# A fused attention and feed-forward kernel on one core: the second product with its operands exchanged and its output transposed

## The chip, the core and the metric

The kernel runs on one core of one Trainium2 chip. The metric is the device time of one execution in microseconds; the median of several runs is compared. What the host does with the arrays before and after the launch isn't part of it.

## What is computed

For 8 batches of 8 heads, 576 tokens and 64 dimensions, an attention without softmax is followed by a norm over each head's 64 values and by a gated feed-forward layer. The 4,608 tokens have 512 values each (8 heads of 64), and the hidden layer has 2,048:

```
kv  = einsum('bhsd,bhse->bhde', k, v)
out = einsum('bhsd,bhde->bhse', q, kv)
x   = out / sqrt(mean(out*out, -1) + 1e-6) * g_norm      # then (b s) x (h d): 4608 x 512
h   = x @ w_in                                           # 4608 x 2048
g   = h * (1 / (1 + exp(-h)))
return g @ w_out                                         # 4608 x 512, float32
```

The weights reach the device as 64-bit words, two 32-bit integers per value, and the kernel makes float32 from them itself.

## The kernel before, in words

**Tiles.** Tokens come in 9 tiles (`NT`) of `TN` = 512. The model's 512 columns (`DM`) are `NP` = 4 pieces of 128, the hidden layer's 2,048 are `NF` = 16 pieces of 128. One step is one pair (token tile `t`, hidden piece `f`); there are 144 of them.

**Precision by parts.** TensorE multiplies `F32R` tiles, each value of which is a rounded float32. Every operand of the two large products is kept as a high part and a low part (the rest), and a product is the sum of three matmuls: high by high, high by low and low by high. For the weights `split_block` (L163) makes the parts: the high one by a ScalarE copy (L166) into `w[:, 0, :]`, the low one by a GpSimd subtraction (L167) into `w[:, 1, :]`. `bits` (L124) before it makes float32 values from the words on VectorE.

**First product**, `products` (L503): for each of the 4 pieces of the model's columns, three matmuls (L507) with a 128 by 128 piece of w_in stationary and 512 tokens of x^T moving (`xl`, then `xh` twice). Twelve matmuls add up in one PSUM bank `hp`: 128 hidden units by 512 tokens.

**Gate**, `gate` (L512): ScalarE reads `hp` twice, into `gh` (F32R, L516) and `gf` (float32, L517), and the low part `gl` = gf - gh is made on VectorE (on GpSimd in the first token tile, L518). Both tiles hold 128 hidden units by 512 tokens.

**Second product**, `project` (L532): for each of four blocks of 128 tokens (`ns`) three matmuls (L537), with 128 columns of `gh`, `gh` and `gl` stationary, and the 512 columns of w_out's piece moving (low part, high part, high part). They add up in the block's own bank `acc`, 128 tokens by 512 columns, over the 16 hidden pieces; so four banks are open through a token tile. These three matmuls are called a group here; a step has four groups. After the last hidden piece the bank is copied to SBUF (`ob`, L542, by ScalarE for odd blocks and VectorE for even ones), and SyncE's queue stores it (L543). In the last token tile the last bank is split into two of 256 columns, one of them from another PSUM pool (`sums_of`, L523), so that the end is shorter.

**Order.** The order is written out by hand (`tc.manual_schedule`). Each step runs, in order: the conversion of weights that falls due (in the first token tile only), the first product, the gate, pieces of the attention for the following batch (`mid_jobs`, L246 and L277 to L279 on TensorE), the second product of the step two before (`LAG` = 2, L727 to L730), and more of the attention. So TensorE takes turns between L507 and L537, with short attention matmuls between in about a third of the steps. After the loop the last two steps' second products are run bank by bank (L733 to L735). Loads and stores all stand in SyncE's queue.

Of the kernel before, what the change touches and what calls it, by code (L numbers as in the profile page):

```python
# [8 lines left out]
F32 = mybir.dt.float32  # L9
# [22 lines left out]
def linear_attention_rms_silu_ffn(  # L32
# [17 lines left out]
    nc = tc.nc  # L50
    B, H, S, D = q.shape
    DM, FF = w_in.shape
    P = 128
    NP = H // 2
    NF = FF // P
    TN = 512
# [14 lines left out]
    ps_acc = ctx.enter_context(tc.tile_pool(name="ps_acc", bufs=4, space=PSUM))  # L71
# [245 lines left out]
    class FirstPair:  # L317
# [43 lines left out]
        def make_out(self):  # L361
            self.ps = self.ps or acc_bank()
            for r in range(4):
                w = slice(r * P, (r + 1) * P)
                nc.tensor.matmul(out=self.ps[:, w], lhsT=self.qT[:, w], rhs=self.kvm, start=True, stop=True)
# [20 lines left out]
    class Rest:  # L386
# [8 lines left out]
        def turn_q(self):  # L395
            self.halves = acc_bank()[0:D, :].rearrange("d (c h n) -> d h c n", h=2, n=64)
            for h in range(2):
                for c in range(NP):
                    nc.tensor.transpose(
                        out=self.halves[:, h, c, :], in_=self.q[:, 2 * c + h, :], identity=ident[:64, :64]  # L400
                    )
# [89 lines left out]
        return ps_h.tile([P, 512], F32, name="hp", tag="h")  # L491

    def acc_bank():
        return ps_acc.tile([P, DM], F32, name="acc", tag="acc")

    at_tags = ["at"]

    def at_bank(tag=None):

        at_tags.append(at_tags.pop(0))  # L500
        return ps_at.tile([P, 512], F32, name="at", tag=tag or at_tags[-1])
# [20 lines left out]

    def sums_of(t):  # L523

        whole, half = slice(0, DM), (slice(0, DM // 2), slice(DM // 2, DM))
        banks = [(acc_bank(), n, whole) for n in range(TN // P)]
        if t == NT - 1:
            last, n, _ = banks.pop()
            banks += [(last, n, half[0]), (at_bank(), n, half[1])]
        return banks  # L530

    def project(t, f, gh, gl, bank, n, cs):  # L532
        w = parts["wo", f]
        ns = slice(n * P, (n + 1) * P)
        bank = bank[:, :cs.stop - cs.start]
        for i, (g, a) in enumerate(((gh, 1), (gh, 0), (gl, 0))):
            nc.tensor.matmul(  # L537
                out=bank, lhsT=g[:, ns], rhs=w[:, a, cs], start=(f == 0 and i == 0), stop=(f == NF - 1 and i == 2)
            )
        if f == NF - 1:  # L540
            ob = tmp.tile([P, S], F32, name="ob", tag="tmp")[:, :cs.stop - cs.start]
            (nc.scalar.copy if n % 2 else nc.vector.tensor_copy)(out=ob, in_=bank)  # L542
            nc.sync.dma_start(out=out[t * TN + n * P:t * TN + (n + 1) * P, cs], in_=ob)  # L543


    first_jobs, mid_jobs, last_jobs, chains = {}, {}, {}, {}
# [38 lines left out]
    with tc.manual_schedule():  # L585
# [4 lines left out]
        for item in ORDER.split():  # L590
            kind, n = item.rstrip("0123456789"), int(item.lstrip("wioqkvbg") or 0)
# [107 lines left out]
        pend, prepped = [], []  # L699
        for t in range(NT):  # L700
            sums = sums_of(t)
            if t == 1:
                at_tags.append("other")
            for f in range(NF):
                g = t * NF + f
                for job in first_jobs.pop(g, ()):
                    job()
                for item in prepped:
                    split_block(*item, nc.scalar.copy)
                prepped = []  # L710
                if t == 0:
                    prepped = [("wi", f + 2)] * (3 <= f + 2 < NF) + [("wo", f)] * (f > 0)
                run(sum((bits(*item) for item in prepped), []), *[call() for call in chains.pop(g, ())])
                if t == 0:
                    for item in [("wi", f + 3)] * (3 < f + 3 < NF) + [("wo", f + 1)] * (1 < f + 1 < NF):
                        magnitude(*item)
                if t == 0 and f < WARM:
                    hp = warm[f]
                    products(hp, t, f, NP - 1)
                else:  # L720
                    hp = h_bank()
                    for c in range(NP):
                        products(hp, t, f, c)
                pend.append(((t, f, *gate(t, hp)), sums))
                for job in mid_jobs.pop(g, ()):
                    job()
                if len(pend) > LAG:  # L727
                    item, olds = pend.pop(0)
                    for old in olds:
                        project(*item, *old)  # L730
                for job in last_jobs.pop(g, ()):
                    job()
        for old in sums:  # L733
            for item, _ in pend:
                project(*item, *old)  # L735


_INS = ["q", "k", "v", "g_norm", "moe_w_in", "moe_w_out"]
_OUT = ((4608, 512), "float32")


# [19 lines left out]
```

## Time and profile before

| | |
|---|---|
| median of 3 runs | 893.68 us (893.66 to 894.28) |
| profiled execution, device time | 893.95 us |
| its span, first to last instruction | 892.1 us |
| mean granted TensorE clock | 0.992 |
| matmuls of the first product (L507) / of the second (L537) | 1,728 / 1,776 |
| stores of the output | 37 |
| bytes read / written in HBM | 45.09 MB / 9.44 MB |

How to read it: PE is TensorE's matmuls and PEld its loads of the stationary operand, which run beside each other; DVE is VectorE, ACT ScalarE, POOL GpSimd and SP SyncE. A row of a group gives line, engine, operation, output <- inputs, the tile size (rows and columns of the array, then output partitions by columns), the count, busy time in us, the mean of one in ns and the idle time before. In such a row `gh` and `gl` stand for the gated units, `wo` for w_out's pieces, `wi` for w_in's, `xh` and `xl` for x^T. A matmul's row lasts until its last column has drained, so that the next one starts before it ends: rows of about 390 ns follow each other every 230 ns or so. The granted clock is the share of TensorE's full speed.

### The profile page before, as it was taken

The page shows a single profiled execution, that of the slowest core. Times are in us where ns is not written, and L with a number is a line of the kernel's source. Part 1 is how long each engine was busy: PE and PEld are TensorE (multiplying, and loading weights), DVE is VectorE, ACT ScalarE, POOL GpSimd, SP SyncE. Part 2 cuts the span into 40 slices and gives each one's busy share as a digit, 9 for nine tenths or more (in the row PEclk, how much of TensorE's full clock was granted, in tenths as well). Part 3 has the DMA queues.
Part 4 walks back from the last instruction along what each step waited for, and adds up shares of the span by engine and source line. Part 5 has one row for each costly group of instructions (what it writes and reads, how often), then busy time and mean ns, then how long its engine had stood idle before and what let it go on. Part 6 is the DMA issues. An engine that isn't in the chain of part 4 may idle for free.

```text
span 892.1 us, 11345 instructions
## 1 busy us (share of the span) xinstructions
PE 871.0 (98%) x4438; PEld 713.1 (80%) x4438; DVE 337.7 (38%) x617; ACT 307.5 (34%) x684; POOL 176.8 (20%) x172
## 2 busy tenths in 40 slices
PE   7879989999999999999999999999999999999998
PEld 6658868888888888888888888888888888888887
DVE  5888894233232423341433233332523141111111
ACT  4567634332343224322432243322432231112121
POOL 1489963101120002101210112010310020000000
PEclk9899989999999999999999999999999999999999
DMA  9869402310052004300431024100400010001001
GB/s 243 257 212 326 117 0 80 87 41 1 11 148 49 0 1 128 80 1 1 116 65 28 1 71 96 41 1 1 127 1 1 1 47 1 1 1 48 0 1 48
DMA packets 108389, 55.26 MB, mean 62 GB/s; under 512 B 76464, under 2 KB 101808, under 8 KB 108336
## 3 DMA queue, kind: packets, MB, share of 16 engines
q1 hardware_dynamic: 108336, 54.54, 22.5%
q8 instruction: 35, 0.57, 0.3%
q14 instruction: 18, 0.15, 0.1%
HBM read 45.09 MB, written 9.44 MB: 61 GB/s over the span
## 4 chain that ended last, share of the span: by engine, by line
PE 87%; DMA 3%; DVE 3%; POOL 3%; issue 2%; SPq 1%; ACT 0%; DVEq 0%; POOLq 0%
PE hp L507 41%; PE acc L537 40%; PE at L246 2%; DMA early_wo<-in_q 1%; DMA wi<-in_moe_w_in 1%; DMA wo<-in_moe_w_out 1%; POOL wi L167 1%; PE at L278 1%; PE at L279 1%; PE at L277 1%; POOL full L120 1%; PE at L537 1%; DMA kv<-in_k 1%; DVE m L476 1%; POOL wo L167 1%
## 5 line engine op out<-in xcount | busy, mean ns | idle before, releaser
L507 PE MATMUL hp<-xh,wi 128*128 128x512 f32 x1144 | 355.4, 392 | 2.1 <-POOL wi L167 2.1
L537 PE MATMUL acc<-wo,gh 128*128 128x512 f32 (+1 forms) x1152 | 355.3, 390 | 1.4 <-POOL wo L167 1.4
L518 DVE TENSOR_TENSOR gl<-gf,gh 128x512 fp32r<-128x512 f32 x128 | 88.6, 692 | 500.5 <-ACT gf L517 500.5
L507 PEld LDWEIGHTS hp<-xh,wi 128*128 128x128 f32 x1144 | 215.9, 189 | 46.0 <-POOL wi L167 3.2
L537 PEld LDWEIGHTS acc<-wo,gh 128*128 128x128 f32 x1152 | 214.8, 188 | 45.8 <-POOL wo L167 1.8
L507 PE MATMUL hp<-xl,wi 128*128 128x512 f32 x572 | 227.8, 398 | 3.5 <-ACT wi L166 3.5
L516 ACT ACTIVATE gh<-hp 128x512 fp32r<-128x512 f32 x143 | 85.5, 598 | 416.8 <-PE hp L507 416.6
L537 PE MATMUL acc<-wo,gl 128*128 128x512 f32 x576 | 222.5, 386 | 0.0
L507 PEld LDWEIGHTS hp<-xl,wi 128*128 128x128 f32 x572 | 108.0, 189 | 26.8 <-ACT wi L166 3.9
L537 PEld LDWEIGHTS acc<-wo,gl 128*128 128x128 f32 x576 | 108.2, 188 | 23.8
L313 POOL TENSOR_TENSOR xl<-o,xh 128x448 fp32r<-128x448 f32 (+7 forms) x56 | 53.2, 951 | 343.5 <-ACT xh L312 343.5
L517 ACT ACTIVATE gf<-hp 128x512 f32<-128x512 f32 x143 | 84.6, 592 | 0.0
L267 POOL TENSOR_TENSOR ql<-qT,qh 128x576 fp32r<-128x576 f32 x28 | 40.1, 1431 | 177.0 <-ACT qh L266 88.5
L283 ACT ACTIVATE sq<-at 128x288 f32<-128x288 f32 x56 | 23.2, 415 | 39.4 <-PE at L279 26.8
L253 ACT COPY kvm<-at 64x64 f32<-64x64 f32 x56 | 11.6, 207 | 59.4 <-PE at L246 59.1
L304 DVE SCALAR_TENSOR_TENSOR o<-o,gcol,yT 128x448 f32<-128x448 f32 (+7 forms) x56 | 31.2, 557 | 2.0
L246 PEld LDWEIGHTS at<-kv 128*64 128x64 f32 (+1 forms) x560 | 20.8, 136 | 12.0 <-issue 9.7
L246 PE MATMUL at<-kv 128*64 128x64 f32 (+1 forms) x560 | 26.5, 231 | 0.0
L312 ACT CAST xh<-o 128x448 fp32r<-128x448 f32 (+7 forms) x56 | 24.8, 442 | 5.0 <-DVE o L304 5.0
L297 DVE STREAM_TRANSPOSE yT<-y 128x448 f32<-128x448 f32 (+7 forms) x56 | 25.9, 463 | 0.0
L167 POOL TENSOR_TENSOR wi<-full,wi 128x512 fp32r<-128x512 f32 x16 | 21.4, 1334 | 21.2 <-ACT wi L166 21.2
L284 ACT COPY o<-at 128x288 f32<-128x288 f32 x56 | 22.7, 406 | 4.0 <-POOL xl L313 4.0
(104 smaller groups left out, 514.5 us busy)
## 6 DMA issues: line engine op xcount, KB each, us to landing
out<-ob SPq DMA_DIRECT2D x35, 256.0 KB, 2.1
wi<-in_moe_w_in SPq DMA_DIRECT2D x16, 512.0 KB, 6.4
wo<-in_moe_w_out SPq DMA_DIRECT2D x16, 512.0 KB, 11.1
qt<-in_q SPq DMA_DIRECT2D x112, 72.0 KB, 3.7
kv<-in_k SPq DMA_DIRECT2D x28, 256.0 KB, 3.1
kv<-in_v SPq DMA_DIRECT2D x28, 256.0 KB, 3.6
kv<-in_k SPq DMA_DIRECT2D x28, 32.0 KB
kv<-in_v SPq DMA_DIRECT2D x28, 32.0 KB
```

The source lines that it names most:

```text
L167: nc.gpsimd.tensor_tensor(out=w[:, 1, :], in0=full, in1=w[:, 0, :].bitcast(F32), op=ALU.subtract)
L246: nc.tensor.matmul(out=self.kv[h], lhsT=self.k[rows, c, :], rhs=self.v[rows, c, :], start=(r == 0), stop=(r == 4))
L267: nc.gpsimd.tensor_tensor(out=self.ql, in0=self.qT, in1=self.qh.bitcast(F32), op=ALU.subtract)
L297: nc.vector.transpose(out=self.yT.rearrange("p (j a) -> p j a", a=32), in_=y[:, a // 32:e // 32].unsqueeze(2).to_broadcast([P, (e - a) // ...
L304: nc.vector.scalar_tensor_tensor(out=self.o[:, a:e], in0=self.o[:, a:e], scalar=gcol, in1=self.yT, op0=ALU.mult, op1=ALU.mult)
L312: nc.scalar.copy(out=th[:, self.c, w], in_=self.o[:, a:e])
L313: nc.gpsimd.tensor_tensor(out=tl[:, self.c, w], in0=self.o[:, a:e], in1=th[:, self.c, w].bitcast(F32), op=ALU.subtract)
L507: nc.tensor.matmul(out=hp[:, :TN], lhsT=w[:, a, fs], rhs=x[:, c, :], start=(c == 0 and i == 0), stop=(c == NP - 1 and i == 2),)
L516: nc.scalar.activation(out=gh, in_=hp[:, :TN], func=AF.Silu)
L517: nc.scalar.activation(out=gf, in_=hp[:, :TN], func=AF.Silu)
L518: (nc.gpsimd if t == 0 else nc.vector).tensor_tensor(out=gl, in0=gf, in1=gh.bitcast(F32), op=ALU.subtract)
L537: nc.tensor.matmul(out=bank, lhsT=g[:, ns], rhs=w[:, a, cs], start=(f == 0 and i == 0), stop=(f == NF - 1 and i == 2))
```

## The change

In the second product the operands change places. A 128 by 128 piece of w_out (high, low, high) is stationary, and the 512 tokens of `gh`, `gh` and `gl` move. A bank now holds 128 of the model's columns by 512 tokens, so the output tensor on the device is out^T, 512 by 4,608; the stores write 128 rows of 512 tokens into it, and the host's code turns the array. The order of the three matmuls in a group changes as well: the high part of w_out is used first and the low part second. In the last token tile the split bank is split by tokens in place of by columns.

```diff
     def acc_bank():
-        return ps_acc.tile([P, DM], F32, name="acc", tag="acc")
+        return ps_acc.tile([P, TN], F32, name="acc", tag="acc")
...
     def sums_of(t):
 
-        whole, half = slice(0, DM), (slice(0, DM // 2), slice(DM // 2, DM))
-        banks = [(acc_bank(), n, whole) for n in range(TN // P)]
+        whole, half = slice(0, TN), (slice(0, TN // 2), slice(TN // 2, TN))
+        banks = [(acc_bank(), n, whole) for n in range(NP)]
...
-        for i, (g, a) in enumerate(((gh, 1), (gh, 0), (gl, 0))):
+        for i, (g, a) in enumerate(((gh, 0), (gh, 1), (gl, 0))):
             nc.tensor.matmul(
-                out=bank, lhsT=g[:, ns], rhs=w[:, a, cs], start=(f == 0 and i == 0), stop=(f == NF - 1 and i == 2)
+                out=bank, lhsT=w[:, a, ns], rhs=g[:, cs], start=(f == 0 and i == 0), stop=(f == NF - 1 and i == 2)
             )
         if f == NF - 1:
             ob = tmp.tile([P, S], F32, name="ob", tag="tmp")[:, :cs.stop - cs.start]
             (nc.scalar.copy if n % 2 else nc.vector.tensor_copy)(out=ob, in_=bank)
-            nc.sync.dma_start(out=out[t * TN + n * P:t * TN + (n + 1) * P, cs], in_=ob)
+            nc.sync.dma_start(out=out[ns, t * TN + cs.start:t * TN + cs.stop], in_=ob)
...
-_OUT = ((4608, 512), "float32")
+_OUT = ((512, 4608), "float32")
...
-    return r.results[0]["out_0"]
+    return np.ascontiguousarray(r.results[0]["out_0"].T)
```

## The prediction

> **What bounds the kernel now.** I read the page first, its busy times and its chain, then the groups of both products, then busy times by stretch, and last the waits of TensorE.
>
> ```profile
> span 892.1 us, 11345 instructions
> PE 871.0 (98%) x4438; PEld 713.1 (80%) x4438; DVE 337.7 (38%) x617; ACT 307.5 (34%) x684; POOL 176.8 (20%) x172
> PE 87%; DMA 3%; DVE 3%; POOL 3%; issue 2%; SPq 1%; ACT 0%; DVEq 0%; POOLq 0%
> ```
>
> TensorE is busy 871.0 of 892.1 us and owns 87% of the chain that ended last. Nothing else is busy over 40%, save PEld, which runs beside PE. The program ran 893.95 us in this execution, 1.85 more than its span. The median of the runs shown is 893.68, so the profiled one is 0.27 long. Whether those 98% hold at every place is read by stretch (columns: length, busy us and instructions of each engine, granted clock, DMA share, GB/s):
>
> ```profile
> 0.00:63.00 63.00, 49.19 (x326) 38.45 (x327) 47.51 (x83) 35.17 (x75) 28.73 (x35) 0.95 0.89 248
> 63.00:128.00 65.00, 61.52 (x323) 50.02 (x321) 57.95 (x88) 38.68 (x81) 54.63 (x54) 0.99 0.50 156
> 128.00:134.00 6.00, 5.45 (x13) 3.88 (x14) 5.83 (x9) 3.20 (x6) 5.02 (x5) 0.51 0.00 0
> 134.00:809.00 675.00, 675.00 (x3386) 553.19 (x3385) 215.33 (x424) 213.94 (x492) 88.42 (x81) 1.00 0.16 42
> 809.00:892.10 83.10, 79.84 (x397) 67.52 (x395) 11.07 (x16) 16.54 (x31) 0.00 (x0) 1.00 0.05 17
> ```
>
> From 134 to 809 us TensorE has not one idle nanosecond: 675.00 of 675.00, at full clock. Before 134 it has gaps, and there the weights' conversion on VectorE and GpSimd decides. The chain in order of time shows it just ahead of 128 us:
>
> ```profile
> 108.32 3.56 DVE m L476
> 120.30 1.24 DVE y L200
> 127.78 1.28 POOL wi L167
> 129.11 5.01 PE hp L507 x11
> ```
>
> PE takes the chain over only at 129.11. What it saves before that is waited away at its longest wait (3.5 us, its products on the ScalarE copy of a w_in piece). So a change of TensorE's pace counts from about 129 us to the end, and there nanosecond for nanosecond.
>
> **The change part by part.** *Number of instructions.* Each group was three matmuls of 512 columns with three weight loads (gh, gh, gl stationary, w_out's piece moving). It stays three of 512 columns with three loads (high, low, high piece of w_out stationary, gh, gh, gl moving). The tile sizes are all 128 by 512, d_model being 512 as TN is. So x4438 stays on PE and on PEld, and nothing is gained or lost by counting.
>
> *Pace of one group.* The two products already do the same amount of work per matmul, one with weights stationary (L507) and one with gated units stationary (L537). Here they are in a steady stretch, 700 to 800 us (busy us, then mean ns of one):
>
> ```profile
> L537 PE MATMUL acc<-wo,gh 128*128 128x512 f32 x150 | 46.7, 393 | 0.0
> L507 PE MATMUL hp<-xh,wi 128*128 128x512 f32 x144 | 44.3, 389 | 0.0
> L537 PE MATMUL acc<-wo,gl 128*128 128x512 f32 x75 | 29.1, 388 | 0.0
> L507 PE MATMUL hp<-xl,wi 128*128 128x512 f32 x72 | 28.0, 389 | 0.0
> ```
>
> A group of the second product is 393 + 393 + 388 = 1174 ns of these, a group of the first 3 x 389 = 1167: **7 ns dearer**. These durations overlap (a matmul ends after the next has begun), so I check with busy time, overlaps counted once, over 98.40 us, which are 18 whole steps. The first row is L537 alone, the second L507 alone:
>
> ```profile
> 699.63:798.03 98.40, 52.38 (x216) 40.57 (x216) 1.00 0.03 11
> 699.63:798.03 98.40, 51.86 (x217) 40.54 (x216) 1.00 0.03 11
> ```
>
> 52.38 - 51.86 = 0.52 us over 18 x 4 = 72 groups is 7.2 ns a group, the same. Both products issue 216 loads of equal busy time there (40.57 and 40.54), so it is not the load itself that is longer. The one difference that I see inside a group is that L537 loads the same stationary tile twice running (gh, gh); L507 alternates high, low, high. The changed L537 alternates as L507 does, with pieces of the same layout. I therefore take L507's pace for it: 7 ns less per group.
>
> *How often.* From 134 us to the end:
>
> ```profile
> L537 PE MATMUL acc<-wo,gh 128*128 128x512 f32 x1016 | 316.5, 393 | 0.0
> L537 PE MATMUL acc<-wo,gl 128*128 128x512 f32 x508 | 197.7, 389 | 0.0
> L537 PE MATMUL acc<-wo,gh 128*128 128x256 f32 x32 | 6.3, 279 | 0.0
> L537 PE MATMUL at<-wo,gh 128*128 128x256 f32 x32 | 6.3, 279 | 0.0
> ```
>
> 508 groups of 512 columns (1016 gh, 508 gl): 508 x 7 = 3.56 us. The last token tile's split bank makes 32 groups of 256 columns; no row shows that shape with weights stationary. Between nothing and the same 7 ns that is 0 to 0.22 us, and I take 0.1. **Sum: -3.66 us.**
>
> *The unknown: gated units as moving operand.* No row shows it. From below: were every matmul as short as the shortest 512-column row (388), a group would be 1164, 10 less than now, -5.1 us. From above: were every one as long as the longest (393), 1179, 5 more than now, +2.5 us. I take 389, as the row nearest in form is L507's, which streams 512 contiguous fp32 values from SBUF, written by ScalarE, past weight pieces.
>
> *Waits.* The wait for gh and gl moves from the weight load to the matmul, and the wait for w_out's halves from the matmul to the load. Behind a waiting one on PE's queue stands the rest of the second product and the next step's first product, and the gate waits for that. Neither wait bites in the steady part:
>
> ```profile
> 504.00 0.60 ACT L516 ACTIVATE gh<-hp 128x512 fp32r<-128x512 f32 x1 [4.14 <-PE hp L507]
> 505.11 0.69 DVE L518 TENSOR_TENSOR gl<-gf,gh 128x512 fp32r<-128x512 f32 x1 [4.03 <-ACT gf L517]
> 514.73 0.62 PE L537 MATMUL acc<-wo,gh 128*128 128x512 f32 x2
> ```
>
> With LAG 2, gl is done at 505.80 and used from 514.73: 8.9 us of cover. Were that cover gone, each step could lose at most what gate and subtraction take, 504.00 to 505.80, 1.8 us. In the first token tile the high half, which ScalarE makes, is now needed first and GpSimd's low half one matmul later:
>
> ```profile
> PE acc L537 <- POOL wo L167: 1.4, 1, 1.4
> PE hp L507 <- ACT wi L166: 3.5, 1, 3.5
> ```
>
> This shortens the one wait of 1.4 us by a matmul's pace (98.40 us / 432 = 0.23 us). It lies before 129 us, so what is late next is the 3.5 us wait, and it counts as nothing (0 to 0.23).
>
> *Copies, stores, queues.* Four evacuations a tile on VectorE and ScalarE keep their size. Each store still moves 128 rows of 2,048 bytes (1,024 in the halves), the rows now 18,432 bytes apart in the output. SP's queue issues as many. Only the last store stands on the path:
>
> ```profile
> 888.88 0.37 ACT L542 COPY ob<-at 128x256 f32<-128x256 f32 x1 [0.28 <-PE at L537]
> out<-ob SPq DMA_DIRECT2D x2, 128.0 KB, 1.8
> out<-ob SPq DMA_DIRECT2D x35, 256.0 KB, 2.1
> ```
>
> I take 1.8 us again for it; twice the bytes took 0.3 us more, so a spread-out target should cost some tenths at most. It could be up to 0.3 dearer, or as much cheaper. The turn of the output is made on the host, outside the measured time.
>
> Forecast: 893.95 - 3.66 = 890.29 for an execution like the profiled one; less its 0.27, **890.0 us**.
>
> *A page that speaks against it.* The Trainium skill, "TensorE: Matmul & The Clock Gate", section Back-to-back issue gap, gives a warm matmul's spacing by its moving columns alone, 512 / 2.4 + 2.5, an estimate of 215.8 ns, whichever operand is stationary. By that rule swapping operands of equal size changes nothing. The trace has 228 ns for the mean spacing and the 7 ns between two products of one size, so the rule does not hold to that precision here.
>
> **The rivals.** *No change, 893.7 us.* The 7 ns belong to something that stays. L537 goes to another PSUM bank after every three matmuls, L507 after twelve. Or gh as an operand costs 4 ns on either side, two of three matmuls each time: 508 x 7 ns stays. For it: the bank hop is the second thing that distinguishes the two lines. Against it: at each step PE also hops from acc to hp, and the products' group holds 3 x 389 all the same. It has 0.21. The page's rule gives the same time.
>
> *Slower, 896.2 us.* The 7 ns are the price of reading the gated units' tiles. These now stream through whole, 512 columns three times a group, where before 128 columns a time were loaded. If each of the three then costs the longest row, 393, a group is 1179: 508 x 5 ns = +2.5 us. If the price went by bytes, four times 7 = 28 ns a group, 21 more than now, +10.7 us, 904.4. It decides from 7 ns a group above L507, where it eats the whole gain. Against it: gl lies in the same pool and its row is the shortest, 388. It has 0.12.
>
> *The half clock.* The wait at 127.8 us is followed by the stretch at 0.51 clock:
>
> ```profile
> 130.55 1.05 PE L507 MATMUL hp<-xh,wi 128*128 128x512 f32 x2
> ```
>
> Two matmuls take 1.05 us there against 0.62 in the steady rows, 0.43 us more, half of it a later start and half a longer end, so about 0.2 us of pace each: some 12 of them are 2.4 us. PE comes to this wait a little earlier (13 steps x 4 x 7 ns = 0.36 us). A second such stretch would give 892.4 (0.04); none, 887.6 (0.03). The Trainium skill, same page, section "What's actually happening", has the clock halved after an idle window of about 3.4 us that runs free; the 3.5 us wait followed by 0.51 agrees.
>
> **How the numbers follow.** Forecast 0.60 (its own range 889.3 to 891.0), no change 0.21, slower 0.12, one more half-clock stretch 0.04, one less 0.03. About 0.2% (1.8 us) is what a measurement of this kernel can tell from no change. Faster by more, under 891.9: 0.60 + 0.03 = 0.63. Within: 0.21 + 0.04 = 0.25. Slower: 0.12. The range takes in both ends of the unknown: 893.68 - 5.1 = 888.6 and 893.68 + 2.5 = 896.2; so 888.5 to 896.3, with only a price by bytes and a vanished half-clock stretch outside.
>
> **What would show it.** Right: L537's 512-column rows all read 389 or 390 in the steady stretch, whichever of gh and gl moves; L537's busy time over 18 steps falls from 52.38 to about 51.86; 134 to 809 us stays full and comes to hold some 3 us more of the program; the counts stay x4438. Wrong: rows of 393, 393, 388 again mean that bank hop or operand made them; rows above 393 that moving gated units are dear. New idle time of PE at L537 with ACT or DVE as releaser would mean that the moved wait bites. A last store that lands later than 1.8 us would show in the tail, after the last matmul.

## The result, and the profile after

The changed kernel takes 902.35 us (median of 6 runs, 900.84 to 903.64) against 893.67 us before (6 runs, 892.25 to 894.98): a ratio of 1.0097, 95% interval 1.0082 to 1.0113. It is about 1% slower, where 0.4% faster was forecast.

The page of the changed kernel, its profiled execution at 903.08 us:

```profile
span 901.3 us, 11344 instructions
PE 878.7 (97%) x4438; PEld 712.0 (79%) x4438; DVE 338.1 (38%) x617; ACT 307.2 (34%) x684; POOL 176.2 (20%) x172
PE 88%; DVE 5%; DMA 3%; POOL 1%; issue 1%; SPq 0%; ACT 0%; DVEq 0%; POOLq 0%; ACTq 0%
```

The counts are the same to the last matmul and load, and PE is as much the bound as it was. The 9.2 us of span are therefore in PE's pace or in its gaps. The same stretches as before:

```profile
63.00:128.00 65.00, 63.56 (x329) 51.09 (x327) 55.71 (x84) 39.43 (x83) 52.11 (x51) 1.00 0.51 155
128.00:134.00 6.00, 3.31 (x8) 2.41 (x9) 5.72 (x9) 3.19 (x6) 4.33 (x5) 0.74 0.00 0
134.00:809.00 675.00, 675.00 (x3353) 546.79 (x3352) 215.44 (x424) 212.01 (x490) 90.18 (x83) 1.00 0.16 41
```

From 134 to 809 us PE is full again, 675.00 of 675.00 at full clock, but it starts 3,353 matmuls there in place of 3,386. No wait came in; each matmul takes longer. The rows of the steady stretch, 700 to 800 us, say which:

```profile
L507 PE MATMUL hp<-xh,wi 128*128 128x512 f32 x146 | 45.4, 391 | 0.0
L537 PE MATMUL acc<-gh,wo 128*128 128x512 f32 x144 | 45.2, 394 | 0.0
L507 PE MATMUL hp<-xl,wi 128*128 128x512 f32 x73 | 28.5, 391 | 0.0
L537 PE MATMUL acc<-gl,wo 128*128 128x512 f32 x72 | 28.4, 394 | 0.0
```

All three matmuls of the second product now read 394, where 393, 393 and 388 stood, and L507, which nobody touched, reads 391 in place of 389. Such a row ends after the next has begun, so the pace is better read from starts. Rows of the changed kernel's order of time (start, length):

```profile
706.83 0.63 PE L537 MATMUL acc<-gh,wo 128*128 128x512 f32 x2
...
709.63 0.39 PE L507 MATMUL hp<-xl,wi 128*128 128x512 f32 x1
...
712.37 0.40 PE L537 MATMUL acc<-gh,wo 128*128 128x512 f32 x1
```

And of the kernel before:

```profile
699.63 0.62 PE L537 MATMUL acc<-wo,gh 128*128 128x512 f32 x2
...
702.38 0.39 PE L507 MATMUL hp<-xl,wi 128*128 128x512 f32 x1
...
705.10 0.39 PE L537 MATMUL acc<-wo,gh 128*128 128x512 f32 x1
```

The twelve matmuls of the second product take 709.63 - 706.83 = 2.80 us, 233.3 ns each, and the first product's twelve 2.74 us; before it was 2.75 and 2.72. Over 18 steps the second product's start comes every 99.72 / 18 = 5.540 us, where it came every 98.40 / 18 = 5.467. Finer, by the starts of each matmul: a group of the second product is 700 ns (687 before), and the first product loses 20 ns at its start, where its second to fifth spacings are 236, 228, 232 and 231 ns in place of 226.7. So a plain step, one without attention matmuls, loses 4 x 13 + 20 = 72 ns (73 by the rounded 5.540 and 5.467).

The chain in order of time tells when PE takes over, first after, then before:

```profile
129.87 1.29 POOL wi L167
131.20 4.21 PE hp L507 x11
135.41 2.81 PE acc L537 x12
```

```profile
134.12 2.07 PE acc L537 x9
```

135.41 - 134.12 = 1.3 us are lost ahead of the steady part. From there to the end it is 901.3 - 135.41 = 765.9 us against 892.1 - 134.1 = 758.0, 7.9 more. By the starts of the rows from the fourteenth second product on, 6.0 of these are the second product's and 1.8 the first's; attention and end have 0.1.

### The profile page after: what moved, and what is told of

The parts are those of the page before. It is cut to its first block, busy times and chain, and to the rows that moved or that the text cites. A ratio compares the mean times of both kernels' runs of the same rounds, so it can differ in the third digit from the quotient of the medians.

```text
span 901.3 us, 11344 instructions
## 1 busy us (share of the span) xinstructions
PE 878.7 (97%) x4438; PEld 712.0 (79%) x4438; DVE 338.1 (38%) x617; ACT 307.2 (34%) x684; POOL 176.2 (20%) x172
## 4 chain that ended last, share of the span: by engine, by line
PE 88%; DVE 5%; DMA 3%; POOL 1%; issue 1%; SPq 0%; ACT 0%; DVEq 0%; POOLq 0%; ACTq 0%
PE hp L507 42%; PE acc L537 41%; PE at L246 3%; DMA early_wo<-in_q 1%; DMA wi<-in_moe_w_in 1%; DMA kv<-in_v 1%; PE at L279 1%; PE at L278 1%; PE at L277 1%; DVE full L158 1%; DVE m L476 1%; PE at L537 1%; DVE conv L155 0%; POOL wi L167 0%; DVE full L139 0%
## 5 line engine op out<-in xcount | busy, mean ns | idle before, releaser
L507 PE MATMUL hp<-xh,wi 128*128 128x512 f32 x1144 | 357.6, 394 | 2.3 <-POOL wi L167 2.3
L537 PE MATMUL acc<-gh,wo 128*128 128x512 f32 (+1 forms) x1152 | 358.2, 391 | 0.9 <-POOL wo L167 0.9
L507 PEld LDWEIGHTS hp<-xh,wi 128*128 128x128 f32 x1144 | 216.6, 190 | 47.8 <-POOL wi L167 3.3
L537 PEld LDWEIGHTS acc<-gh,wo 128*128 128x128 f32 x1152 | 214.4, 188 | 50.1 <-POOL wo L167 1.2
L507 PE MATMUL hp<-xl,wi 128*128 128x512 f32 x572 | 228.4, 399 | 3.7 <-ACT wi L166 3.3
L537 PE MATMUL acc<-gl,wo 128*128 128x512 f32 x576 | 225.4, 391 | 0.0
L507 PEld LDWEIGHTS hp<-xl,wi 128*128 128x128 f32 x572 | 108.1, 189 | 27.9 <-ACT wi L166 3.7
L537 PEld LDWEIGHTS acc<-gl,wo 128*128 128x128 f32 x576 | 107.9, 187 | 25.6
```

Source lines behind the costliest of these rows:

```text
L507: nc.tensor.matmul(out=hp[:, :TN], lhsT=w[:, a, fs], rhs=x[:, c, :], start=(c == 0 and i == 0), stop=(c == NP - 1 and i == 2),)
L537: nc.tensor.matmul(out=bank, lhsT=w[:, a, ns], rhs=g[:, cs], start=(f == 0 and i == 0), stop=(f == NF - 1 and i == 2))
```

## The experiments

**The theories.** The prediction's two explanations were the repeated stationary tile and the bank hop; it had the gated units' tiles themselves as a rival. A fourth came after the result and stands in no row of the trace: the *place* of the operands in SBUF. By the addresses that the program is built with, w_in's and w_out's pieces and x^T start 192 bytes past a multiple of 512 in each partition, and gh and gl start 128 past. So the first product reads two operands in line (difference of moving and stationary start 0), the second product before had +64 (w_out's pieces moving), and the changed one has -64. Below, "in line" means a difference of 0 modulo 512: the 128-column pieces of a stationary tile lie 512 bytes apart, so 512 is taken as the period. Whether a shorter one would do, 256 above all, was not tried for a whole product.

**1. The gated units in line.** The changed kernel, with

```diff
+    pad = ctx.enter_context(tc.tile_pool(name="pad", bufs=1))
     gp = ctx.enter_context(tc.tile_pool(name="gp", bufs=LAG + 1))
...
+    nc.gpsimd.memset(pad.tile([P, 16], F32, name="space"), 0.0)
```

> The changed kernel with 64 unused bytes per partition put ahead of the gated units' tiles, so that gh and gl start 192 bytes past a multiple of 512, as w_out's pieces and x^T do, in place of 128 past. In the changed kernel a steady step lasts 5.540 us, its second product 2.800 (233.3 ns a matmul) and its first 2.740. If the address of the moving tile relative to the stationary one sets the pace, the second product falls to about 2.720 us (226.7 ns a matmul, the first product's pace), the step to about 5.44 us, and the whole by some 12 us to about 890 us. If bank hops, the repeated use of the same moving tile, or the place of the tiles at the high end of SBUF set it, all stays: 2.800, 5.540 and about 902 us.

It took 891.18 us, beside 892.56 for the kernel before on the same chip. The rows of 700 to 800 us (L539 is the second product, two lines further down):

```profile
L509 PE MATMUL hp<-xh,wi 128*128 128x512 f32 x150 | 46.2, 389 | 0.0
L539 PE MATMUL acc<-gh,wo 128*128 128x512 f32 x145 | 44.7, 389 | 0.0
L509 PE MATMUL hp<-xl,wi 128*128 128x512 f32 x75 | 29.2, 389 | 0.0
L539 PE MATMUL acc<-gl,wo 128*128 128x512 f32 x73 | 28.4, 389 | 0.0
```

Four times 389: 64 unused bytes make gated units as cheap to move as x^T. In order of time:

```profile
705.52 0.39 PE L509 MATMUL hp<-xl,wi 128*128 128x512 f32 x1
...
708.24 0.62 PE L539 MATMUL acc<-gh,wo 128*128 128x512 f32 x2
...
710.96 0.39 PE L509 MATMUL hp<-xl,wi 128*128 128x512 f32 x1
```

2.72 us for each product: the first one's 20 ns have gone as well.

**2. No bank hops.** The changed kernel, in which a step's four groups add up in one bank, `first` taking the place of `f == 0` as the start of a sum; the sums go to the wrong blocks.

```diff
-    def project(t, f, gh, gl, bank, n, cs):
+    def project(t, f, gh, gl, bank, n, cs, first=None):
+        first = f == 0 if first is None else first
...
-                    for old in olds:
-                        project(*item, *old)
+                    for j, old in enumerate(olds):
+                        if item[0] < NT - 1 and item[1] < NF - 1:
+                            project(*item, olds[item[1] % 4][0], *old[1:], first=(item[1] < 4 and j == 0))
+                        else:
+                            project(*item, *old)
```

> The changed kernel, but in each step but a tile's last the four groups of the second product add up in one PSUM bank (the step's number modulo four), so that twelve matmuls in a row write one bank as in the first product; the sums go to the wrong blocks, the work and the number of matmuls stay. The last token tile is as it was. If the hop to another bank after three matmuls costs the time, the second product falls from 2.800 to about 2.72 us a step in the first eight tiles and the whole by about 11 us. If the moving tile's address or its place costs it, nothing changes: 2.800 us a step and about 902 us.

901.43 us, and the same rows as the changed kernel:

```profile
L538 PE MATMUL acc<-gh,wo 128*128 128x512 f32 x146 | 45.8, 394 | 0.0
L538 PE MATMUL acc<-gl,wo 128*128 128x512 f32 x73 | 28.8, 394 | 0.0
```

The bank hop costs nothing here.

**3. x^T moves in the second product.** The changed kernel, with the result of the gate unused:

```diff
-        for i, (g, a) in enumerate(((gh, 0), (gh, 1), (gl, 0))):
+        mh, ml = xh[t][:, 0, :], xl[t][:, 0, :]
+        for i, (g, a) in enumerate(((mh, 0), (mh, 1), (ml, 0))):
```

> The changed kernel, but the second product's moving operand is the first 512 columns of x^T (high, high, low part) in place of gh, gh, gl; the gate still runs, its result is not used. The same three tiles still repeat in all four groups, and the bank hops stay. If the address or the place of the gated units' tiles sets the pace, the second product falls to about 2.72 us a step and the whole to about 890 us. If the repeated moving tile or the bank hop sets it, it stays at 2.800 us and about 902 us.

889.57 us:

```profile
L538 PE MATMUL acc<-xh,wo 128*128 128x512 f32 x147 | 45.3, 389 | 0.0
L538 PE MATMUL acc<-xl,wo 128*128 128x512 f32 x73 | 28.4, 389 | 0.0
```

Hops and repeats are all still there, and the pace is the first product's. What remains is the tile that moves, or where it lies; run 1 says where it lies.

**4. The kernel before, in line.** The same two lines as in run 1, put into the kernel before.

> The kernel before with the same 64 unused bytes ahead of the gated units' tiles. There gh and gl are stationary, a group of the second product takes 687 ns and a step 5.467 us. If the relative address sets the pace, the 7 ns a group go: 680 ns a group, 5.44 us a step, the whole about 3.5 us faster, near 890 us. If loading the same stationary tile twice running made the 7 ns, they stay: 5.467 us a step and about 893.7 us.

890.42 us, beside 892.56. The 7 ns a group are gone, with gh still loaded twice running:

```profile
L509 PE MATMUL hp<-xh,wi 128*128 128x512 f32 x151 | 46.6, 389 | 0.0
L539 PE MATMUL acc<-wo,gh 128*128 128x512 f32 x145 | 44.7, 389 | 0.0
L539 PE MATMUL acc<-wo,gl 128*128 128x512 f32 x72 | 28.0, 389 | 0.0
```

So my explanation of the 7 ns by the repeated stationary tile falls.

**5. Place, or relation?** The changed kernel with 64 bytes ahead of all tiles: the difference stays -64, while gh and gl start 192 past, as in run 1.

```diff
+    nc.gpsimd.memset(const.tile([P, 16], F32, name="space"), 0.0)
     kvm = [const.tile([P, P], F32, name=f"kvm{i}") for i in range(H // 2)]
```

> The changed kernel with 64 unused bytes ahead of every tile: w_out's pieces and x^T start 256 bytes past a multiple of 512 and gh and gl 192 past; the difference between them is -64, as in the changed kernel, but gh and gl start where they did in the fast first run. If the difference between moving and stationary tile counts, all stays: 2.800 us for the second product of a step, 2.740 for the first, about 902 us. If the start address of the moving tile by itself counts (192 good, 128 bad), the second product falls to 2.72 us.

900.47 us, with 2.80 us for the second product and 2.74 for the first:

```profile
L538 PE MATMUL acc<-gh,wo 128*128 128x512 f32 x146 | 46.0, 394 | 0.0
L538 PE MATMUL acc<-gl,wo 128*128 128x512 f32 x73 | 28.8, 394 | 0.0
```

It is the relation of moving to stationary start that counts, not the start by itself.

**6. The price on the other product.** Run 1's kernel with x^T put 64 short of w_in's pieces:

```diff
+    xpad = ctx.enter_context(tc.tile_pool(name="xpad", bufs=1))
     xpool = ctx.enter_context(tc.tile_pool(name="xpool", bufs=2))
...
-    nc.gpsimd.memset(pad.tile([P, 16], F32, name="space"), 0.0)
+    nc.gpsimd.memset(pad.tile([P, 32], F32, name="space"), 0.0)
+    nc.gpsimd.memset(xpad.tile([P, 112], F32, name="xspace"), 0.0)
```

> The price put on the other product: the changed kernel with the gated units' tiles in line with w_out's pieces, but x^T 64 bytes short of w_in's pieces (448 unused bytes ahead of x^T, 128 ahead of the gated units' tiles). If the difference between a product's own moving and stationary tiles sets its pace, the first product takes 2.800 us a step in place of 2.720 and the second 2.720 to 2.740; the step is 5.54 us and the time about 902 us, as in the changed kernel. If there is something in the gated units or in the second product itself, the first stays at 2.72 and the time is near 891 us.

903.75 us. Its order of time (L541 is the second product, L511 the first):

```profile
706.91 0.62 PE L541 MATMUL acc<-gh,wo 128*128 128x512 f32 x2
...
709.65 0.39 PE L511 MATMUL hp<-xl,wi 128*128 128x512 f32 x1
...
712.46 0.39 PE L541 MATMUL acc<-gh,wo 128*128 128x512 f32 x1
```

The changed kernel in a mirror: 2.74 us for the second product, 2.81 for the first (2.800 by the starts to the nanosecond). The price has nothing to do with gated units or with the second product.

**7 to 9. Other differences.** Two runs give each buffer of gh and gl another difference; here is the first, and the second has 24 in place of 32 in its last line:

```diff
-        gh = gp.tile([P, TN], F32R, name="gh")
+        gh = gp.tile([P, TN + 16], F32R, name="gh")[:, :TN]
...
-        gl = gp.tile([P, TN], F32R, name="gl")
+        gl = gp.tile([P, TN + 16], F32R, name="gl")[:, :TN]
...
-    nc.gpsimd.memset(pad.tile([P, 16], F32, name="space"), 0.0)
+    nc.gpsimd.memset(pad.tile([P, 32], F32, name="space"), 0.0)
```

> The changed kernel with 128 unused bytes ahead of the gated units' tiles and each of them 64 bytes longer, so that the three buffers of gh start 64, 128 and 192 bytes further on than w_out's pieces and x^T, modulo 512, and those of gl 256, 320 and 384; each step takes the next buffer. So far a difference of 0 gave 226.7 ns a matmul and one of -64 gave 233.3. If the pace hangs on the difference, the matmuls of L537 show different spacings in three steps that take turns, between 226.7 and 233.3 or beyond. If only -64 is bad, all are at 226.7 and the time is near 890 us. If only a difference of 0 is good, all are at about 233 and the time is near 902 us.

> As the run with six phases, but the differences between the gated units' tiles and w_out's pieces are 32, 96 and 160 bytes for gh and 224, 288 and 352 for gl. If the pace hangs on the difference in steps of 64 bytes, rows differ from those of the run with 64 to 384; if in another way, the spacing over both runs shows it. A spacing below 226.7 ns at any difference would give a version that beats both kernels.

901.21 and 902.39 us. The second product takes 2.800, 2.778 and 2.778 us in the three steps that take turns (gh and gl at 64 and 256; 192 and 384; 128 and 320), and 2.801, 2.807 and 2.796 in the other run (32 and 224; 160 and 352; 96 and 288). None comes near 2.720. The third is run 1's kernel with gh 4, 8 or 16 bytes further on:

```diff
+    at4 = [1, 2, 4]
...
+        at4.append(at4.pop(0))
-        gh = gp.tile([P, TN], F32R, name="gh")
+        gh = gp.tile([P, TN + 128], F32R, name="gh")[:, at4[0]:at4[0] + TN]
```

> The changed kernel with the gated units' tiles in line with w_out's pieces (difference 0 modulo 512), except that gh starts 4, 8 or 16 bytes further on, in steps that take turns; gl stays at 0. If lines of 64 bytes or more are what counts, all three steps keep 226.7 ns a matmul and the time is near 891 us. If the exact start counts, gh's matmuls lie above 226.7 ns by an amount that differs between the three steps, with a step of up to 5.54 us and a time of up to 902 us. A spacing below 226.7 would be a better place than 0.

903.61 us: 2.841 us at 4 bytes, 2.806 at 8 and 2.773 at 16. The exact start counts, and the smallest offset, 4 bytes, is the worst of all that were tried. In these three runs gh and gl start apart from each other too, so the price of one difference by itself can't be read from them. The Trainium skill, "SBUF — State Buffer", section Specifications (TRN2), gives SBUF lines of 16 bytes and a penalty for each new line; 4 and 8 bytes dearer than 16 fits that, but whole lines cost as well: 2.773 us at 16 bytes, and 2.800 in the changed kernel, 64 short.

**10 and 11. In line, timed.** Runs 1 and 4 again.

> The first run's kernel (changed, 64 unused bytes, difference 0), timed. The first run gave a step of 5.440 us against 5.467 before: 27 ns by some 127 steps is 3.4 us, so about 890.2 us against 893.7, ratio 0.996. If the gain were chance of one run, the ratio would be 1.000 within its interval.

> The fourth run's kernel (before, 64 unused bytes, difference 0), timed. Both orders of operands have the same step of 5.440 us there, so it should be as fast as the changed kernel in line, about 890.2 us, ratio 0.996, and the change by itself be worth nothing either way once the tiles are in line.

The changed kernel in line takes 889.63 us (7 runs), ratio to the kernel before 0.995, interval 0.9932 to 0.9967; the kernel before in line 889.80 us (9 runs), 0.9948, 0.9931 to 0.9965. Both beat both kernels of this case, and the 0.17 us between them is less than the runs of either scatter. Once the tiles are in line, the change is worth nothing that these runs can tell; the 64 bytes are worth 0.5% on one side and 1.4% on the other.

**12. The sign.** The changed kernel with gh and gl 64 further on than w_out's pieces (run 1's edit with 32 in place of 16).

> The changed kernel with 128 unused bytes ahead of the gated units' tiles, so that they start 64 bytes further on than w_out's pieces, in place of 64 short. In the kernel before, w_out's pieces moved 64 bytes further on than the stationary gh and gl, and a group took 687 ns; in the changed kernel gh and gl move 64 bytes short of the stationary pieces, and a group takes 700. If the sign of moving less stationary start is what makes 687 of one and 700 of the other, a group takes about 687 ns here, a step 5.467 us, the whole about 893.7. If the order of operands makes it, it takes 700 ns or more and the whole is near 902 us.

Half and half. A settled group is 232 + 226 + 229 = 687 ns, as with +64 in the kernel before, so the sign makes that. But the run took 901.08 us. Its order of time:

```profile
707.67 0.40 PE L509 MATMUL hp<-xl,wi 128*128 128x512 f32 x1
...
710.44 0.63 PE L539 MATMUL acc<-gh,wo 128*128 128x512 f32 x2
...
713.21 0.40 PE L509 MATMUL hp<-xl,wi 128*128 128x512 f32 x1
```

The first product takes 2.77 us here though its own operands are in line, 50 ns too many, and the second product's first group 703 ns. So there are two prices: a settled one of a product's own difference, and one at each change of product. The second was nil in the four kernels in whose two products the moving tiles start alike (before, runs 1, 3 and 4). It was 20 ns a step in the changed kernel and in runs 2, 5 and 6. It isn't the stationary tiles' starts: those of the two products differ in the kernel before and agree in run 12. That the moving tiles' starts make it is read from these cases, not tried by itself, and it isn't the whole rule. In run 9 gl, the last to move, starts like x^T, and the first product lost 21 to 39 ns all the same. In runs 7 and 8 it lost 24 to 48 ns, but nothing (2.720 us) after the steps of run 7 with gl at 256, where gl's own spacing was 228 ns; so 256 may be nearly as good as 0, which isn't shown. And in the kernel before too a first product right after attention matmuls takes a few spacings to settle (236, 228, 232 and 231 ns from the second on).

## Why the prediction was wrong

**What bounds the kernel: right.** PE is full from 134 to 809 us in both kernels, and what the matmuls lost there, 72 ns in a plain step, went into the time in full.

**Counts: right.** x4438 and x4438 again.

**Pace of one group: wrong, and this is the step that failed.** The 7 ns were real, and the rows showed them. But "the one difference that I see inside a group is that L537 loads the same stationary tile twice running" was a guess from one pair of rows that differ in several ways at once. Run 4 took the 7 ns away and left the repeat. The difference that counted isn't in any row of the trace: where the tiles start. With it goes "I take 389, as the row nearest in form is L507's": L507's 389 is the pace of two operands in line, not of weights stationary. In place of -7 ns a group it was +13 (700 for 687), and run 1, with one edit of 64 bytes, gave the -7 after all (680 for 687).

**The bounds of the unknown: too narrow.** From above I took 393 three times, +5 a group. A pace in which all three are bad together was in no row before. Durations that overlap also hid its size: the rows went from 1174 to 1182, 8 ns, the spacing from 687 to 700, 13 ns. And nothing in the sum stood for the first product, which lost 20 ns in a plain step.

**How often: right** (508 groups). In the steps with attention matmuls less is lost, so that the second product's 6.0 us are a little under 508 x 13 = 6.6.

**Waits: right.** No new releaser of L537 appeared, and the one named got shorter, 1.4 to 0.9 us:

```profile
PE hp L507 <- ACT wi L166: 3.3, 1, 3.3
PE acc L537 <- POOL wo L167: 0.9, 1, 0.9
```

**Stores: right.** The last matmul begins at 897.72, and the span ends 3.6 us later; before it was 888.56 and 3.5. That the rows lie further apart in HBM shows in a tenth at most:

```profile
out<-ob SPq DMA_DIRECT2D x35, 256.0 KB, 2.2
```

**The start: not as forecast.** I had it at nothing; the profiled run lost 1.3 us there. But the start differs by more than that from run to run. By the matmuls' starts the fourteenth second product begins at 133.96 us before and at 135.25 after. In runs 2 and 5, which have the changed kernel's pace, it begins at 133.58 and 132.29, and in runs 1 and 10, which are one kernel, at 134.61 and 132.94. So nothing shows that the 1.3 us are the change's.

**The rivals.** "No change" by bank hop: run 2 rules the hop out as the cost. The Trainium skill's formula of spacing by columns alone ("TensorE: Matmul & The Clock Gate", Back-to-back issue gap) is given there for an isolated matmul, beside the remark that in a real kernel the loads set the spacing too. It would have every one of these matmuls alike; the runs have 226.7 to 237 ns for one shape. "Slower" was right in sign, and the time came out between its 896.2 and its 904.4. That was luck, since its mechanism was wrong: reading the gated units' tiles has no price of its own (runs 1 and 6). The price goes by the relation between both operands. So the sign that I had set for this rival, rows above 393, came true and would have misled. The half-clock stretch near 130 us was there in both kernels, and it was shorter after the change (0.74 of the clock from 128 to 134 us in place of 0.51), so it doesn't account for the loss.

What in the memory or in TensorE's reading makes this relation matter stays open: the runs show that it does, at which differences and how much, and not by what conflict. Nor do they tell whether the stationary tile that counts is the one in the array or the next one, loaded meanwhile; inside a product both start alike here. The Trainium skill ("TensorE: Matmul & The Clock Gate", Step-by-step: what each phase is for) has loading and moving on two separate ports, so that the load takes no read bandwidth from the running matmul. The loads' rows kept their length (187 to 188 ns), but the matmuls' pace hangs on where both operands start, so separate ports don't make the two independent in this kernel.

## What to carry to other kernels

Before an explanation is given to a few nanoseconds between two rows of one shape, list all in which the rows differ, the tiles' start addresses too; a pad of 64 bytes is the cheapest experiment there is. Where TensorE is the bound and the operands are F32R as here, start moving and stationary tiles alike modulo 512 bytes, and the moving tiles of products that take turns alike as well: small odd-sized tiles allocated ahead of a pool shift it silently. That holds for what was tried here, 512 columns against 128 by 128. And give an operand in a role that no row shows a range wider than the rows of the other roles.

## What the runs showed of the hardware

I had not expected the pace of a matmul of 512 float32 columns to depend on its operands' start addresses: 226.7 ns at a difference of 0, 229 on average at +64, 233.3 at -64, and up to 237 on average (2.841 us for twelve) where two of three were 4 bytes off. Nor had I expected that a product whose own operands are in line is slowed at its start, by 20 to 50 ns, by the product that ran before it.
